# Decode attention over a window of the cache: output copies on the vector engine, one q-projection, another order of the last loads

## The chip, the cores and the metric

The kernel runs on one core of a Trainium2 chip. The metric is the device time of one execution in microseconds; for several executions the median is given. Beside these runs there is one profiled execution, with a trace of every engine and DMA queue.

## The reference

It is one decoding step of grouped-query attention over a window of a key and value cache: 32 sequences (B), one query position, width D = 512, 32 query heads (H) on 8 key/value heads (G), head size 128, cache length 2048. Only the last W = 512 positions are used. All tensors are bf16.

```python
W = min(4096, max(256, Sk // 4))                      # 512
q = (x @ wq).reshape(B, Sq, Hq, Dh)                   # to (B, Hq, 1, Dh)
k = repeat(k_cache[:, :, Sk - W:, :], 4 per head)
v = repeat(v_cache[:, :, Sk - W:, :], 4 per head)
p = softmax((q @ k^T) * Dh ** -0.5)
out = (p @ v).reshape(B, Sq, Hq * Dh) @ wo            # (32, 1, 512)
```

Per sequence 1 MB of K and 1 MB of V are read; wq and wo are 4 MB each. Together it is 75.5 MB.

## The kernel before

The program is written by hand for each engine: each engine runs a fixed list of instructions in order, and semaphores tie the lists together. The sequences are numbered b = 0 to 31 and grouped in 8 blocks kb of four (`NBLK`).

**Loads.** SP issues every load on one queue. K goes into 4 slots (`NK`), V into 10 (`NV`). The order is x, K0, wq, then K(b) and V(b-3) by turns (`VLAG = 3`), wo after V7, and at the end V29, V30, V31. `load_k(b)` waits until the transposes of sequence b-4 are done, and `load_v(b)` until pv of sequence b-10 is done. wo overwrites wq in `wbuf`; `load_wo` waits until the q-projection is over and evacuated.

**Front.** x is transposed on TensorE. `qproj(half)` computes q for 16 heads each, as 64 matmuls into the one PSUM bank `m_ps`; `qt_evac(half)` on ScalarE scales it and copies it into `qT_sb`. The bank holds (head, sequence), `qT_sb` holds (sequence, head), so the copy writes with a step of 32 elements. The second half waits on PE until the first has been evacuated.

**For each sequence s.** TensorE transposes K of sequence s+2 (`transposes`, 32 transposes of 128x128 in four groups). VectorE evacuates three groups into `kT_sb` and ScalarE one (`evac`). `scores(s)` multiplies 8 weight tiles `L` with the transposed K and adds up four sequences in one PSUM half of `sc_ps`, so that 128 partitions hold 4 sequences x 32 heads. `lcopy(blk)` on VectorE puts the q of a block into the places of `L` that aren't zero.

**For each block kb.** VectorE takes the maximum and its negation (`max_block`), ScalarE the exponential with its sum (`exp_block`), VectorE normalises (`norm_block`), TensorE transposes the probabilities (`ptrans`), ScalarE evacuates them (`pt_evac`), and TensorE multiplies with V (`pv`, 128 matmuls of 4 columns). `ot_evac(kb)` copies the result, 128 columns of `m_ps`, into `oT_sb`; this runs on ScalarE and writes with a step of 32 elements, since `oT_sb` holds (head, sequence). At the end `oproj` adds up 32 matmuls of 512 columns, with `oT_sb[:, h * B:(h + 1) * B]` as weights and wo as moving operand, and `out_evac` on ScalarE copies the result out.

**Where the order is set.** TensorE's order is one loop over s = 0 to 39: `transposes(s+2)`, `scores(s)`, then `ptrans(kb)` at s = 4kb+4 and `pv(kb)` at s = 4kb+5. So pv(6) comes at s = 29, between scores(29) and scores(30), and ptrans(7) and pv(7) come at s = 32 and 33. VectorE and ScalarE have loops over b with tasks before and after the evacuations of b: `ot_evac(kb)` before those of b = 4kb+8, `max_block(kb)` and `exp_block(kb)` after those of b = 4kb+5, `norm_block(kb)` before those of b = 4kb+6.

Of the kernel before, what the change touches and what calls it, by code (L numbers as in the profile page):

```python
# [5 lines left out]
B = 32  # L6
D = 512
H = 32
# [25 lines left out]
def bass_standalone__sliding_block_cached__sampling_kernel(  # L34
# [9 lines left out]
    with ExitStack() as ctx:  # L44
# [7 lines left out]
        L = [sb(f"L{i}", [128, 32 * 128], BF16) for i in range(2)]  # L52
        qT_sb = sb("qT_sb", [128, B * H], BF16)
        x_sb = sb("x_sb", [128, D], BF16)
# [4 lines left out]
        pT_sb = [sb(f"pT{i}", [128, W], BF16) for i in range(2)]  # L59
        oT_sb = sb("oT_sb", [128, H * B], BF16)  # L60
        out_sb = sb("out_sb", [128, D], BF16)
# [24 lines left out]
        sem_act_pT = sem("sem_act_pT")  # L86
        sem_act_oT = sem("sem_act_oT")
        sem_act_misc = sem("sem_act_misc")
        sem_dve_kT = sem("sem_dve_kT")
        sem_dve_sm = sem("sem_dve_sm")  # L90
        sem_dve_P = sem("sem_dve_P")
        sem_dve_L = sem("sem_dve_L")
        sem_dve_loc = sem("sem_dve_loc")

# [13 lines left out]
        @block.sync  # L108
        def _(sp):
            def load_k(b):  # L110
                slot = b % NK
                if b >= NK:
                    sp.wait_ge(sem_pe_kT, 4 * (b - NK) + 4)
                src = k_cache[b, :, SK - W:, :].rearrange("g (p r) d -> p g (r d)", p=128)
                dst = kbuf[slot][:, :].rearrange("p (g x) -> p g x", g=G)
                sp.dma_start(dst, src).then_inc(sem_k[slot], 16)  # L116

            def load_v(b):
                slot = b % NV
                if b >= NV:  # L120
                    sp.wait_ge(sem_pe_pv, b - NV + 1)
                src = v_cache[b, :, SK - W:, :].rearrange("g (p r) d -> p g (r d)", p=128)
                dst = vbuf[slot][:, :].rearrange("p (g x) -> p g x", g=G)
                sp.dma_start(dst, src).then_inc(sem_v[slot], 16)  # L124

            def load_wo():
                sp.wait_ge(sem_pe_misc, 3)
                sp.wait_ge(sem_act_misc, 3)
                sp.dma_start(
                    wbuf[:, :].rearrange("p (h n) -> p h n", h=H),  # L130
                    wo.rearrange("(h p) n -> p h n", p=128),
                ).then_inc(sem_wo, 16)

            sp.dma_start(x_sb[0:B, :], x.rearrange("b o d -> (b o) d")).then_inc(sem_x, 16)
            load_k(0)
            sp.dma_start(  # L136
                wbuf[:, :].rearrange("p (t n) -> p t n", t=DT),
                wq.rearrange("(t p) n -> p t n", p=128),
            ).then_inc(sem_wq, 16)
            for b in range(1, B):  # L140
                load_k(b)
                if b >= VLAG:
                    load_v(b - VLAG)
                if b == WO_AFTER:
                    load_wo()
            for b in range(B - VLAG, B):
                load_v(b)
            sp.wait_ge(sem_act_misc, 4)
            sp.dma_start(out.rearrange("b o d -> (b o) d"), out_sb[0:B, :]).then_inc(sem_out, 16)
            sp.wait_ge(sem_out, 16)  # L150
# [13 lines left out]
        def _(pe):  # L164
# [6 lines left out]

            def qproj(half):
                if half == 0:
                    pe.wait_ge(sem_wq, 16)
                    pe.wait_ge(sem_act_misc, 1)
                else:
                    pe.wait_ge(sem_act_misc, 2)
                for hh in range(16):
                    h = 16 * half + hh
                    for t in range(DT):  # L180
                        ins = pe.matmul(  # L181
                            m_ps[:, hh * B:(hh + 1) * B],
                            wbuf[:, t * (H * DH) + h * DH: t * (H * DH) + (h + 1) * DH],
                            xT_sb[:, t * B:(t + 1) * B],
                            start=(t == 0),
                            stop=(t == DT - 1),
                        )
                ins.then_inc(sem_pe_misc, 1)
# [18 lines left out]
            def scores(b):  # L207
                blk, bl = divmod(b, 4)
                half = blk % 2
                if bl == 0:  # L210
                    pe.wait_ge(sem_dve_L, blk + 1)
                    if blk >= 2:
                        pe.wait_ge(sem_act_exp, blk - 1)
                for g in range(G):
                    n = 4 * b + g // 2
                    if g % 2 == 0:
                        pe.wait_ge(evac_sem(n), evac_count(n))
                    ins = pe.matmul(  # L218
                        sc_ps[:, half * 512:(half + 1) * 512],
                        L[blk % 2][:, (bl * 8 + g) * 128:(bl * 8 + g + 1) * 128],  # L220
                        kT_sb[b % NKT][:, g * W:(g + 1) * W],
                        start=(bl == 0 and g == 0),
                        stop=(bl == 3 and g == G - 1),
                    )
                ins.then_inc(sem_pe_scb, 1)
# [9 lines left out]
            def pv(kb):  # L235
                pe.wait_ge(sem_act_pT, kb + 1)
                reg = kb % 4
                if kb == 0:
                    pe.wait_ge(sem_act_misc, 3)
                if kb >= 4:  # L240
                    pe.wait_ge(sem_act_oT, kb - 3)
                for bl in range(4):
# [14 lines left out]
            def oproj():  # L257
                pe.wait_ge(sem_act_oT, NBLK)
                pe.wait_ge(sem_wo, 16)
                pe.wait_ge(sem_act_exp, NBLK - 1)  # L260
                for h in range(H):
                    ins = pe.matmul(  # L262
                        sc_ps[0:B, 0:512],
                        oT_sb[:, h * B:(h + 1) * B],
                        wbuf[:, h * D:(h + 1) * D],
# [7 lines left out]
            transposes(1)  # L273
            qproj(0)
            qproj(1)
            for s in range(0, B + 8):
# [4 lines left out]
                for kb in range(NBLK):  # L281
                    if s == 4 * kb + 3 + LAG1:
                        ptrans(kb)
                    if s == 4 * kb + 3 + LAG2:
                        pv(kb)
# [3 lines left out]
        def _(act):  # L289
# [3 lines left out]

            def qt_evac(half):
                act.wait_ge(sem_pe_misc, 2 + half)
                act.activation(  # L296
                    qT_sb[:, :].rearrange("p (b h) -> p h b", b=B)[:, 16 * half:16 * half + 16, :],
                    m_ps[:, :].rearrange("p (h b) -> p h b", h=16),
                    ACTF.Copy,
                    scale=scale,  # L300
                ).then_inc(sem_act_misc, 1)

# [36 lines left out]

            def ot_evac(kb):  # L340
                act.wait_ge(sem_pe_pv, 4 * kb + 4)
                if kb >= 1:
                    act.wait_ge(sem_act_oT, kb)
                reg = kb % 4
                act.activation(  # L345
                    oT_sb[:, :].rearrange("p (h b) -> p b h", h=H)[:, 4 * kb:4 * kb + 4, :],
                    m_ps[:, reg * 128:(reg + 1) * 128].rearrange("p (b h) -> p b h", b=4),
                    ACTF.Copy,
                ).then_inc(sem_act_oT, 1)

            def out_evac():
                act.wait_ge(sem_pe_misc, 4)
                act.activation(out_sb[0:B, :], sc_ps[0:B, 0:512], ACTF.Copy).then_inc(sem_act_misc, 1)  # L353

            def block_tasks_pre(b):
                for kb in range(NBLK):
                    if b == 4 * kb + 5 + LAG2 + 1:
                        ot_evac(kb)

# [9 lines left out]
            evac(1, 3)  # L369
            qt_evac(0)  # L370
            qt_evac(1)
            for b in range(2, B):
# [3 lines left out]
            for b in range(B, B + 12):  # L376
                block_tasks_pre(b)
                block_tasks_post(b)
            out_evac()

        @block.vector
        def _(dve):
# [16 lines left out]
            def lcopy(blk):  # L399
                if blk == 0:  # L400
                    dve.wait_ge(sem_act_misc, 3)
                    dve.wait_ge(sem_pool, 4)
# [3 lines left out]
                dst = bass.AP(L[blk % 2], 0, [[32 * 128, 128], [1056, 4], [132, 8], [1, 4]])  # L406
                src = bass.AP(qT_sb, blk * 128, [[B * H, 128], [32, 4], [4, 8], [1, 4]])
                dve.tensor_copy(dst, src).then_inc(sem_dve_L, 1)  # L408
# [11 lines left out]
            def norm_block(kb):  # L420
# [6 lines left out]
                dve.tensor_scalar(P_sb[kb % 2][:, :], E_sb[:, :], rs[kb % 2][:, 0:1], None, ALU.mult).then_inc(sem_dve_P, 1)  # L427

            def E(b):
                for c in range(3):  # L430
                    evac(b, c)

            def block_tasks_pre(b):
                for kb in range(NBLK):
                    if b == 4 * kb + 6:
                        norm_block(kb)

            def block_tasks_post(b):
# [10 lines left out]
            for b in range(2, B):  # L449
                block_tasks_pre(b)  # L450
                E(b)
                block_tasks_post(b)
            for b in range(B, B + 8):
                block_tasks_pre(b)
                block_tasks_post(b)


# [26 lines left out]
```

## Time and profile before

| | |
|---|---|
| median of 6 runs | 243.61 us (241.43 to 245.88) |
| profiled execution | 242.48 us |
| its span, from the first to the last instruction | 240.4 us |
| mean granted TensorE clock | 0.844 |
| PE / weight loads busy | 177.6 us / 136.0 us |
| VectorE / ScalarE busy | 74.8 us / 56.5 us |
| HBM read | 75.53 MB, mean 314 GB/s over the span |
| K load, from issue to landing (median) | 12.0 us |
| longest waits | ScalarE for K transposes 104.5 us, VectorE for them 65.2 us, PE for K loads 49.3 us |

The span lies 2.1 us under the time of the same execution. Busy times are sums of instruction durations; matmuls overlap, so a busy PE isn't one at its peak. "PEld" is the weight load of a matmul, which has a row of its own. A wait is the idle time of an engine ahead of an instruction, with what ended it. "The chain that ended last" follows the work back from the last instruction, at each step to what released it.

### The profile page before, as it was taken

How to read it: one execution, taken by the hardware profiler on the slowest of the kernel's cores; microseconds unless marked ns; L12 is line 12 of the kernel's file. 1: busy time of each engine (PE TensorE's matmuls, PEld its weight loads, DVE VectorE, ACT ScalarE, POOL GpSimd, SP SyncE). 2: the span in 40 equal slices, each digit the busy share in tenths (PEclk: the TensorE clock that was granted, in tenths of full speed). 3: DMA queues.
4: the chain of work that ended last, by engine and by line, in shares of the span. 5: the costliest groups of instructions: out<-in, count | busy, mean ns of one | idle time of the engine just before them, and what ended most of it. 6: DMA issues, size and time to landing. Idle time of an engine off the chain costs nothing.

```text
span 240.4 us, 5498 instructions
## 1 busy us (share of the span) xinstructions
PE 177.6 (74%) x2477; PEld 136.0 (57%) x2500; DVE 74.8 (31%) x136; ACT 56.5 (24%) x69; POOL 7.6 (3%) x8
## 2 busy tenths in 40 slices
PE   0506599969981059996958699869986998497695
PEld 0506577657750056874946478647854785284632
DVE  0303054640460030365315413641364136131100
ACT  2100543412240001242203212221232123211200
POOL 8300000000000000000000000000000000000000
PEclk9965789987897557799979977987798779889769
DMA  6999999999999999999999999999999999993000
GB/s 202 423 386 348 350 348 350 349 348 348 350 350 348 349 348 350 350 348 350 350 348 348 349 348 350 348 348 349 348 348 350 348 348 348 345 341 110 3 3 5
DMA packets 71320, 75.92 MB, mean 316 GB/s; under 512 B 1089, under 2 KB 70785, under 8 KB 70785
## 3 DMA queue, kind: packets, MB, share of 16 engines
q1 hardware_dynamic: 71296, 75.57, 97.8%
q8 instruction: 20, 0.33, 0.6%
q14 instruction: 4, 0.02, 0.0%
HBM read 75.53 MB, written 0.03 MB: 314 GB/s over the span
## 4 chain that ended last, share of the span: by engine, by line
DMA 56%; PE 37%; ACT 2%; SPq 2%; issue 1%; DVE 1%; DVEq 0%
DMA kbuf<-in_k_cache_dram 56%; PE kT_ps L204 16%; PE m_ps L248 8%; PE sc_ps L218 8%; PE sc_ps L262 4%; PE m_ps L181 1%; SPq L124 1%; ACT qT_sb L296 1%; ACT oT_sb L345 0%; DVE mx L416 0%; SPq L116 0%; ACT pT L338 0%; ACT out_sb L353 0%; SPq L136 0%; DVE P L427 0%
## 5 line engine op out<-in xcount | busy, mean ns | idle before, releaser
L204 PE MATMUL kT_ps<-ident,kbuf 128*128 128x128 bf16 x1024 | 81.2, 253 | 49.3 <-DMA kbuf<-in_k_cache_dram 49.3
L204 PEld LDWEIGHTS kT_ps<-ident,kbuf 128*128 128x128 bf16 x1024 | 76.1, 116 | 56.4 <-DMA kbuf<-in_k_cache_dram 54.5
L394 DVE COPY kT<-kT_ps 128x1024 bf16<-128x1024 bf16 x96 | 62.6, 686 | 116.1 <-PE kT_ps L204 65.2
L218 PE MATMUL sc_ps<-kT,L 128*128 128x512 bf16 x233 | 60.8, 401 | 1.8 <-DVE kT L394 0.4
L312 ACT ACTIVATE kT<-kT_ps 128x1024 bf16<-128x1024 bf16 x32 | 32.7, 1023 | 111.9 <-PE kT_ps L204 104.5
L218 PEld LDWEIGHTS sc_ps<-kT,L 128*128 128x128 bf16 x256 | 25.0, 103 | 26.6 <-issue 5.6
L248 PEld LDWEIGHTS m_ps<-pT,vbuf 128*128 128x128 bf16 x1024 | 27.1, 97 | 2.5 <-ACT pT L338 0.9
L248 PE MATMUL m_ps<-pT,vbuf 128*128 128x4 bf16 x1024 | 27.2, 165 | 0.7 <-ACT pT L338 0.7
L345 ACT ACTIVATE oT_sb<-m_ps 128x128 bf16<-128x128 f32 x8 | 5.8, 730 | 34.7 <-PE m_ps L248 34.7
L416 DVE TENSOR_REDUCE mx<-sc_ps 128x1 f32<-128x512 f32 x8 | 5.5, 691 | 16.6 <-PE sc_ps L218 16.6
L262 PE MATMUL sc_ps<-wbuf,oT_sb 128*32 128x512 bf16 x32 | 8.9, 448 | 0.8 <-ACT oT_sb L345 0.8
L324 ACT ACTIVATE E_sb<-sc_ps,nmx 128x512 f32<-128x512 f32 x8 | 5.5, 687 | 14.6 <-DVE nmx L418 14.6
L262 PEld LDWEIGHTS sc_ps<-wbuf,oT_sb 128*32 128x32 bf16 x32 | 3.5, 111 | 5.9 <-issue 2.5
L338 ACT ACTIVATE pT<-pT_ps 128x512 bf16<-128x512 bf16 x8 | 4.8, 597 | 7.4 <-PE pT_ps L232 7.4
L181 PE MATMUL m_ps<-xT_sb,wbuf 128*128 128x32 bf16 x128 | 3.7, 185 | 2.5 <-ACT qT_sb L296 2.5
L296 ACT ACTIVATE qT_sb<-m_ps 128x512 bf16<-128x512 f32 x2 | 4.8, 2406 | 2.6 <-PE m_ps L181 2.6
L181 PEld LDWEIGHTS m_ps<-xT_sb,wbuf 128*128 128x128 bf16 x128 | 3.6, 102 | 2.6 <-ACT qT_sb L296 2.6
L232 PEld LDWEIGHTS pT_ps<-ident,P 128*128 128x128 bf16 x32 | 2.4, 98 | 4.6 <-DVE P L427 3.0
L232 PE MATMUL pT_ps<-ident,P 128*128 128x128 bf16 x32 | 3.1, 219 | 2.5 <-DVE P L427 2.5
L408 DVE COPY L<-qT_sb 128x128 bf16<-128x128 bf16 x8 | 1.5, 188 | 8.6 <-ACT qT_sb L296 8.6
L427 DVE TENSOR_SCALAR P<-E_sb,rs 128x512 bf16<-128x512 f32 x8 | 3.9, 487 | 0.3
L160 POOL MEMSET L<- 128x4096 bf16 x1 | 3.5, 3511 | 0.0
(15 smaller groups left out, 11.1 us busy)
## 6 DMA issues: line engine op xcount, KB each, us to landing
kbuf<-in_k_cache_dram SPq DMA_DIRECT2D x32, 1024.0 KB, 12.0
vbuf<-in_v_cache_dram SPq DMA_DIRECT2D x32, 1024.0 KB, 12.0
wbuf<-in_wq_dram SPq DMA_DIRECT2D x1, 4096.0 KB, 15.2
wbuf<-in_wo_dram SPq DMA_DIRECT2D x1, 4096.0 KB, 20.9
x_sb<-in_x_dram SPq DMA_DIRECT2D x1, 32.0 KB, 1.8
out_dram<-out_sb SPq DMA_DIRECT2D x1, 32.0 KB, 1.5
```

Source lines behind the costliest of these rows:

```text
L181: ins = pe.matmul(m_ps[:, hh * B:(hh + 1) * B], wbuf[:, t * (H * DH) + h * DH: t * (H * DH) + (h + 1) * DH], xT_sb[:, t * B:(t + 1) * B], ...
L204: ins = pe.transpose(dst, src, ident[:, :])
L218: ins = pe.matmul(sc_ps[:, half * 512:(half + 1) * 512], L[blk % 2][:, (bl * 8 + g) * 128:(bl * 8 + g + 1) * 128], kT_sb[b % NKT][:, g * W ...
L232: ins = pe.transpose(pT_ps[:, j * 128:(j + 1) * 128], P_sb[kb % 2][:, j * 128:(j + 1) * 128], ident[:, :])
L248: ins = pe.matmul(m_ps[:, reg * 128 + bl * 32 + 4 * g: reg * 128 + bl * 32 + 4 * g + 4], vbuf[vslot][:, g * W + j * 128: g * W + (j + 1) * ...
L262: ins = pe.matmul(sc_ps[0:B, 0:512], oT_sb[:, h * B:(h + 1) * B], wbuf[:, h * D:(h + 1) * D], start=(h == 0), stop=(h == H - 1),)
L296: act.activation(qT_sb[:, :].rearrange("p (b h) -> p h b", b=B)[:, 16 * half:16 * half + 16, :], m_ps[:, :].rearrange("p (h b) -> p h b", ...
L312: act.activation(kT_sb[b % NKT][:, c * 1024:(c + 1) * 1024], kT_ps[:, bank * 1024:(bank + 1) * 1024], ACTF.Copy,).then_inc(sem_act_kT, 1)
L324: act.activation(E_sb[:, :], sc_ps[:, half * 512:(half + 1) * 512], ACTF.Exp, bias=nmx[kb % 2][:, 0:1], scale=1.0, accum_out=ssum[kb % 2][ ...
L345: act.activation(oT_sb[:, :].rearrange("p (h b) -> p b h", h=H)[:, 4 * kb:4 * kb + 4, :], m_ps[:, reg * 128:(reg + 1) * 128].rearrange("p ...
L394: dve.tensor_copy(kT_sb[b % NKT][:, c * 1024:(c + 1) * 1024], kT_ps[:, bank * 1024:(bank + 1) * 1024],).then_inc(sem_dve_kT, 1)
L416: dve.tensor_reduce(mx[kb % 2][:, 0:1], sc_ps[:, half * 512:(half + 1) * 512], AXX, ALU.max).then_inc(sem_dve_loc, 1)
```

## The change

It has these parts:

- The q-projection is done in one go: 128 matmuls into both banks of `sc_ps` (1024 f32 columns), and one `qt_evac` on ScalarE. `qT_sb` now holds (head, sequence), so the copy is plain. `lcopy` reads `qT_sb` with a step of 32 elements instead.
- `ot_evac` and `out_evac` move from ScalarE to VectorE. `oT_sb` now holds (sequence, head), so that copy is plain too; `oproj` reads its weights from `oT_sb` with a step of 32 elements instead.
- SP's order is built as a list, and K31 is put directly behind K30, ahead of V27.
- On TensorE pv(6) moves from s = 29 to s = 31, behind scores(31). Its `ot_evac(6)` on VectorE comes at b = 33, ahead of the tasks after b = 33, among which is `max_block(7)`.

```diff
 # SP
-            for b in range(1, B):
-                load_k(b)
-                if b >= VLAG:
-                    load_v(b - VLAG)
-                if b == WO_AFTER:
-                    load_wo()
-            for b in range(B - VLAG, B):
-                load_v(b)
+            for b in range(1, B):
+                order.append(("k", b))
...
+            order.remove(("k", B - 1))
+            order.insert(order.index(("k", B - 2)) + 1, ("k", B - 1))
...
 # TensorE
-            def qproj(half):
+            def qproj():
...
-                            m_ps[:, hh * B:(hh + 1) * B],
+                            sc_ps[:, h * B:(h + 1) * B],
...
             def pv(kb):
-                    pe.wait_ge(sem_act_oT, kb - 3)
+                    pe.wait_ge(sem_dve_oT, kb - 3)
...
             def oproj():
-                        oT_sb[:, h * B:(h + 1) * B],
+                        bass.AP(oT_sb, h, [[B * H, 128], [H, B]]),
...
-                    if s == 4 * kb + 3 + LAG2:
+                    pv_at = 4 * kb + 3 + LAG2
+                    if kb == NBLK - 2:
+                        pv_at = B - 1
+                    if s == pv_at:
                         pv(kb)
 # ScalarE
-            def qt_evac(half):
-                act.wait_ge(sem_pe_misc, 2 + half)
-                act.activation(
-                    qT_sb[:, :].rearrange("p (b h) -> p h b", b=B)[:, 16 * half:16 * half + 16, :],
-                    m_ps[:, :].rearrange("p (h b) -> p h b", h=16),
-                    ACTF.Copy,
-                    scale=scale,
-                ).then_inc(sem_act_misc, 1)
+            def qt_evac():
+                act.wait_ge(sem_pe_misc, 2)
+                act.activation(qT_sb[:, :], sc_ps[:, :], ACTF.Copy, scale=scale).then_inc(sem_act_misc, 1)
...
-            def ot_evac(kb):
...
-            def out_evac():
...
 # VectorE
             def lcopy(blk):
-                src = bass.AP(qT_sb, blk * 128, [[B * H, 128], [32, 4], [4, 8], [1, 4]])
+                src = bass.AP(qT_sb, blk * 4, [[H * B, 128], [1, 4], [4 * B, 8], [B, 4]])
...
+            def ot_evac(kb):
+                dve.wait_ge(sem_pe_pv, 4 * kb + 4)
+                if kb >= 1:
+                    dve.wait_ge(sem_dve_oT, kb)
+                reg = kb % 4
+                dve.tensor_copy(oT_sb[:, kb * 128:(kb + 1) * 128], m_ps[:, reg * 128:(reg + 1) * 128]).then_inc(sem_dve_oT, 1)
+
+            def out_evac():
+                dve.wait_ge(sem_pe_misc, 3)
+                dve.tensor_copy(out_sb[0:B, :], sc_ps[0:B, 0:512]).then_inc(sem_dve_out, 1)
...
             def block_tasks_pre(b):
                 for kb in range(NBLK):
                     if b == 4 * kb + 6:
                         norm_block(kb)
+                    ot_at = 4 * kb + 5 + LAG2 + 1
+                    if kb == NBLK - 2:
+                        ot_at = B + 1
+                    if b == ot_at:
+                        ot_evac(kb)
```

More of the change, by code (lines that the diff above doesn't have):

```diff
@@ L52, in bass_standalone__sliding_block_cached__sampling_kernel @@
         L = [sb(f"L{i}", [128, 32 * 128], BF16) for i in range(2)]
-        qT_sb = sb("qT_sb", [128, B * H], BF16)
+        qT_sb = sb("qT_sb", [128, H * B], BF16)
         x_sb = sb("x_sb", [128, D], BF16)
@@ L59, in bass_standalone__sliding_block_cached__sampling_kernel @@
         pT_sb = [sb(f"pT{i}", [128, W], BF16) for i in range(2)]
-        oT_sb = sb("oT_sb", [128, H * B], BF16)
+        oT_sb = sb("oT_sb", [128, B * H], BF16)
         out_sb = sb("out_sb", [128, D], BF16)
@@ L86, in bass_standalone__sliding_block_cached__sampling_kernel @@
         sem_act_pT = sem("sem_act_pT")
-        sem_act_oT = sem("sem_act_oT")
         sem_act_misc = sem("sem_act_misc")
@@ L92, in bass_standalone__sliding_block_cached__sampling_kernel @@
         sem_dve_L = sem("sem_dve_L")
+        sem_dve_oT = sem("sem_dve_oT")
+        sem_dve_out = sem("sem_dve_out")
         sem_dve_loc = sem("sem_dve_loc")
@@ L126, in load_wo @@
             def load_wo():
-                sp.wait_ge(sem_pe_misc, 3)
-                sp.wait_ge(sem_act_misc, 3)
+                sp.wait_ge(sem_pe_misc, 2)
+                sp.wait_ge(sem_act_misc, 2)
                 sp.dma_start(
@@ L139, in _ @@
             ).then_inc(sem_wq, 16)
+            order = []
             for b in range(1, B):
-                load_k(b)
+                order.append(("k", b))
                 if b >= VLAG:
-                    load_v(b - VLAG)
+                    order.append(("v", b - VLAG))
                 if b == WO_AFTER:
+                    order.append(("wo", 0))
+            for b in range(B - VLAG, B):
+                order.append(("v", b))
+            order.remove(("k", B - 1))
+            order.insert(order.index(("k", B - 2)) + 1, ("k", B - 1))
+            assert len(order) == len(set(order)) == 2 * B
+            for kind, b in order:
+                if kind == "k":
+                    load_k(b)
+                elif kind == "v":
+                    load_v(b)
+                else:
                     load_wo()
-            for b in range(B - VLAG, B):
-                load_v(b)
-            sp.wait_ge(sem_act_misc, 4)
+            sp.wait_ge(sem_dve_out, 1)
             sp.dma_start(out.rearrange("b o d -> (b o) d"), out_sb[0:B, :]).then_inc(sem_out, 16)
@@ L170, in xT @@
                 ins.then_inc(sem_pe_misc, 1)
-            def qproj(half):
[L173 to L179, printed above, removed]
+            def qproj():
+                pe.wait_ge(sem_wq, 16)
+                pe.wait_ge(sem_act_misc, 1)
+                for h in range(H):
                     for t in range(DT):
                         ins = pe.matmul(
-                            m_ps[:, hh * B:(hh + 1) * B],
+                            sc_ps[:, h * B:(h + 1) * B],
                             wbuf[:, t * (H * DH) + h * DH: t * (H * DH) + (h + 1) * DH],
@@ L211, in scores @@
                     pe.wait_ge(sem_dve_L, blk + 1)
+                    if blk == 0:
+                        pe.wait_ge(sem_act_misc, 2)
                     if blk >= 2:
@@ L237, in pv @@
                 reg = kb % 4
-                if kb == 0:
-                    pe.wait_ge(sem_act_misc, 3)
                 if kb >= 4:
-                    pe.wait_ge(sem_act_oT, kb - 3)
+                    pe.wait_ge(sem_dve_oT, kb - 3)
                 for bl in range(4):
@@ L257, in oproj @@
             def oproj():
-                pe.wait_ge(sem_act_oT, NBLK)
+                pe.wait_ge(sem_dve_oT, NBLK)
                 pe.wait_ge(sem_wo, 16)
@@ L273, in _ @@
             transposes(1)
-            qproj(0)
-            qproj(1)
+            qproj()
             for s in range(0, B + 8):
@@ L338, in pt_evac @@
                 act.activation(pT_sb[kb % 2][:, :], pT_ps[:, 0:W], ACTF.Copy).then_inc(sem_act_pT, 1)
-            def ot_evac(kb):
[L341 to L349, printed above, removed]
-            def out_evac():
-                act.wait_ge(sem_pe_misc, 4)
-                act.activation(out_sb[0:B, :], sc_ps[0:B, 0:512], ACTF.Copy).then_inc(sem_act_misc, 1)
             def block_tasks_pre(b):
-                for kb in range(NBLK):
-                    if b == 4 * kb + 5 + LAG2 + 1:
-                        ot_evac(kb)
+                pass
             def block_tasks_post(b):
@@ L369, in _ @@
             evac(1, 3)
-            qt_evac(0)
-            qt_evac(1)
+            qt_evac()
             for b in range(2, B):
@@ L378, in _ @@
                 block_tasks_post(b)
-            out_evac()
         @block.vector
@@ L400, in lcopy @@
                 if blk == 0:
-                    dve.wait_ge(sem_act_misc, 3)
+                    dve.wait_ge(sem_act_misc, 2)
                     dve.wait_ge(sem_pool, 4)
@@ L452, in _ @@
                 block_tasks_post(b)
-            for b in range(B, B + 8):
+            for b in range(B, B + 12):
                 block_tasks_pre(b)
                 block_tasks_post(b)
+            out_evac()
 _INS = ['x', 'k_cache', 'v_cache', 'wq', 'wo']
```

## The prediction, made before the changed kernel was run

> **What bounds the kernel now.** I read three views in this order: the slices of the page, the chain of work that ended last, and the timeline of the last 50 us. First the slices (40 of them, 6 us each):
>
> ```profile
> PEclk9965789987897557799979977987798779889769
> DMA  6999999999999999999999999999999999993000
> GB/s 202 423 386 348 350 348 350 349 348 348 350 350 348 349 348 350 350 348 350 350 348 348 349 348 350 348 348 349 348 348 350 348 348 348 345 341 110 3 3 5
> ```
>
> From the fourth slice to slice 36 the loads run at about 349 GB/s without a hole. The TensorE rows of the waits view say the same from the other side: PE waits 49.3 us in all for kbuf. So until about 220 us the kernel is a copy from HBM, and work saved there only makes PE wait longer. After the last load there is a tail with no traffic. It is read from the end of the chain (start us, us, what):
>
> ```profile
> 196.03 13.25 DMA kbuf<-in_k_cache_dram
> ...
> 209.32 3.32 PE kT_ps L204 x32
> ...
> 212.65 1.29 PE sc_ps L218 x6
> ...
> 214.37 3.19 PE m_ps L248 x128
> ...
> 217.63 3.41 PE sc_ps L218 x15
> ...
> 221.07 0.70 DVE mx L416
> ...
> 224.62 3.50 PE m_ps L248 x128
> ...
> 228.15 0.73 ACT oT_sb L345
> ...
> 228.93 8.94 PE sc_ps L262 x32
> ...
> 237.89 0.59 ACT out_sb L353
> ```
>
> K of sequence 31 lands at 209.28. Behind it stand its transposes, scores(29), all of pv(6), scores(30) and (31), the softmax of block 7, pv(7), the output projection and the copy out. The last V is not in this chain: its issue began at 209.5 and landed 11.6 us later, at 221.1, before pv(7) starts. **The tail hangs on when K31 lands, not on when the loads end.** The timeline shows what fills the queue and PE before that:
>
> ```profile
> 193.08 2.90 SPq L124 DMA_DIRECT2D vbuf<-in_v_cache_dram  x1
> 196.03 2.79 SPq L116 DMA_DIRECT2D kbuf<-in_k_cache_dram  x1
> 202.10 1.96 PE L204 MATMUL kT_ps<-ident,kbuf 128*128 128x128 bf16 x32 [1.10 <-DMA kbuf<-in_k_cache_dram]
> 205.62 0.39 PE L232 MATMUL pT_ps<-ident,P 128*128 128x128 bf16 x4
> 209.32 3.32 PE L204 MATMUL kT_ps<-ident,kbuf 128*128 128x128 bf16 x32 [3.31 <-DMA kbuf<-in_k_cache_dram]
> ```
>
> V27 is issued at 193.08 and lands 12.0 us later, at 205.1; K31 is next. PE idles 3.31 us for it.
>
> **Part 1, the front: merged q-projection, plain qT copy, lcopy.** Two strided ScalarE copies of 2.41 us, with PE idle 2.5 us between the halves, become one plain copy of 1024 columns, 1.02 us by the row of the 1024-column kT evacuation. Scores(0) start some 3.5 us earlier than 32.44. I cost this at nothing: wq, K1, K2 and K3 have long been issued then, and the later issues stand back to back (K6 at 32.82 follows V2's, which began at 29.86 and took 2.92), so no load starts sooner. PE then waits longer for K4, K5 and on. If loads were not the bound, the 3.5 us would be a gain. `lcopy` now reads qT with a step of 32 elements: between today's 0.19 us and 0.73 us (the strided ScalarE row below), eight times, in idle VectorE time (busy 31%); uncovered it could cost 8 x 0.54 = 4.3 us, but each runs many microseconds ahead of its block's scores. load_wo's two waits end earlier and it stands behind ten loads: nothing.
>
> **Part 2, oT and out copies from ScalarE to VectorE.** The row of L345 is 730 ns. VectorE has no such copy in the trace. Its rows are 691 ns for reducing 512 f32 from PSUM and 686 ns for copying 1024 bf16; one f32 column per 1.04 ns and a fixed 0.155 us fit the first, so 128 columns are 0.29 us. Bounds: 0.22 (twice that rate) and 0.73 (no better than ScalarE). For blocks 0 to 5 the copy stands ahead of E(4kb+8) on VectorE and waits for pv(kb), but on PE pv(kb) is issued before the transposes that E needs, so the evacuations behind it lose no time: after the pv that ended at 192.75 the next one started at 193.72. The last one is on the path: 0.73 becomes 0.29, **-0.44**. The copy to out_sb, 512 f32 columns, takes 0.69 by the reduction's row against 0.59 on ScalarE: **+0.10** (0.42 to 0.73 as bounds).
>
> **Part 3, the output projection reads oT with a step.** Its weights, [128 x 32], now step 32 elements (64 bytes) from column to column. No strided weight load is in the trace. The nearest row is ScalarE's strided writes with that step: 2406 ns for 512 and 730 ns for 128 columns, 4.36 ns a column; plain ScalarE copies (597 for 512, 1023 for 1024) make 0.83. [...] By the row a load would be 32 x (4.36 - 0.83) = 0.11 us longer than its 97 ns, 0.21 us. Laid open it costs 32 x 0.11 = 3.6 us. But in the last 5 us of the projection one matmul ends every 0.216 us (22 loads over 4.63 us in the timeline) and the loads already run beside the previous matmul, so 0.21 us just fits. I take 0 (bounds 0 and +3.6; a gain is excluded, since the loads are hidden already).
>
> **Part 4, K31 before V27.** The order by index is now K30, K31, V27 to V31. SP issues K31 at 193.08 instead of 196.03. Its wait is for the transposes of sequence 27, which ended at 187.1, so nothing behind it on SP is held. It lands where V27 did, at 205.1; V27 where K31 did, at 209.28; V28 to V31 as before (212.2, 215.0, 218.0, 221.1).
>
> **Part 5, pv(6) behind scores(31), and its copy ahead of max_block(7).** PE now goes: ptrans(6) ends 206.01. Transposes(31) start at 206.05, since K31 is there. They take 1.96, not 3.32: the slow ones ran at a granted clock of 0.5 after the idle 3.3 us, and now there is no idle. Scores(29) 1.89, to 209.9; scores(30) and (31) 3.41, to 213.3. V27 is there, so pv(6) runs 3.19, to 216.5. On VectorE the new copy of pv(6) is *in front of* max_block(7). So the max, its negation, the exponential, the normalisation, ptrans(7) and pv(7) all queue behind it although the scores were ready at 213.3: moving pv(6) off PE's path puts it back through VectorE. Copy 0.29, to 216.85. From the start of the max to the start of pv(7) the chain took 3.55 (221.07 to 224.62): pv(7) starts at 220.4. All but V31 have landed, and its quarter comes at 223.0: no wait. pv(7) 3.50, to 223.9; copy 0.29; projection from 224.3 instead of 228.93.
>
> **Sum.** K31 earlier, 209.32 - 206.05 = 3.27; transposes(31) at full clock, 1.36; the copy in front of the max, -0.33; last copy, +0.44; out copy, -0.10: **4.6 us**. The span goes from 240.4 to 235.8. The profiled execution took 242.48, 2.1 more than its span, so it would take 237.9. It lies 1.1 below the median of the six runs, 243.61; taken from that median, 4.6 us leave **239.0**.
>
> [...] The granted clock, microsecond by microsecond, is 0.5 from 225.9 to 232.7 and 1.0 after, so the projection spent its first 3.8 us at half rate and took 8.94, where 32 x 0.216 is 6.9. All changes near the end sit on one grid of 3.41 us (191.7, 195.1, 208.8, 212.2, 225.9, 232.7). [...] By the row I keep 8.94. [...]
>
> **Rivals.**
> (a) *K31 doesn't land earlier*, because the queue holds it back. Then the chain is today's plus 0.33 minus 0.44 plus 0.10: 243.6. The back-to-back issues speak against it.
> (b) *Weight loads laid open*: +3.6, so 242.6. For: the cover fits by a hair. Against: loads stand beside matmuls in this trace.
> (c) *Slower: strided loads neither overlap nor stay short.* Each matmul of the projection then takes 0.216 + 0.097 + 32 x 4.36 ns = 0.45 us, 14.5 for 32, with 2.0 for the cold start 16.5: 7.5 more than today, net +2.9, 246.5. It decides once a matmul with its load takes over (8.94 + 4.6 - 2.0) / 32 = 0.36 us.
> (d) *The softmax is not held by the new copy.* Then V31 sets the end: 221.1 + 0.9 for its quarter is 222.0 instead of 223.9: 237.1. The order on VectorE speaks against it.
>
> **How the numbers follow.** Forecast 0.73, rival (a) 0.07, (b) 0.09, (c) 0.07, (d) 0.04. A measurement of this kernel can tell about 1%, 2.4 us, from no change. Faster by more than that: forecast, (d), and the cheaper half of (b), 0.80; within 1%: 0.13; slower: 0.07. The forecast's own range, with the clock's -1.2 to +0.5, copies up to 0.4 dearer and a median that wanders by some 0.7, is 237.0 to 240.4; to leave out no more than 2 in 10 it goes up to 241.5.
>
> **What would show it.** Right: the waits for kbuf end near 206; no PE idle ahead of transposes(31); pv(6) between scores(31) and ptrans(7); the max of block 7 right after the oT copy at about 216.8; projection from 224.3; loads ending near 220 as now. Wrong: a spacing of over 0.25 us between projection matmuls at full clock, K31 landing after 207, the max starting near 213, or holes in the load rate before slice 34.

## The result and the profile after

The changed kernel takes 238.87 us (median of 10 runs, 237.58 to 240.32); the kernel before takes 243.74 us in the same series. The ratio is 0.982, with a 95% interval of 0.979 to 0.985: about 4.4 us of 243.7 are gone. The medians are over all runs, while the ratio leaves out runs more than 1.5% above the fastest of their kernel, which here only the kernel before has. The forecast was 239.0.

The slices of the page show that the stream of loads is as before, and only the tail behind it is shorter:

```profile
DMA  6999999999999999999999999999999999996000
GB/s 199 425 389 348 349 349 349 349 348 349 348 350 349 347 349 349 350 348 350 348 350 349 349 348 348 349 348 349 350 346 350 347 349 348 349 334 225 4 3 6
```

The rate stays at 349 GB/s from the fourth slice on. A slice is now 5.96 us, so the traffic ends at the same time, near 220 us.

The profiled execution took 240.12 us (span 238.3). That is only 2.4 us below the profiled execution of before, while the medians lie 4.9 apart. A profile is one execution: the one of before was 1.3 us under its median, this one 1.3 us over. I therefore read the changed kernel from two profiles, this one and the one of the repeat (e1). First the end of the chain in this one (start us, us, what):

```profile
202.49 2.44 PE kT_ps L212 x32
204.94 0.22 issue
205.16 2.69 PE sc_ps L228 x7
207.85 0.22 PE pT_ps L242 x4
208.07 1.79 PE kT_ps L212 x32
...
215.04 3.25 PE m_ps L256 x128
...
218.52 0.69 DVE mx L402
...
222.27 3.59 PE m_ps L256 x128
...
226.23 9.50 PE sc_ps L270 x32
```

K31 is no longer in it: its issue began at 193.5 and it landed 12.0 us later, at 205.5, before PE asked for it at 208.07. V27 was issued at 196.4 and landed at 209.4. But transposes(31) still start 2 us later than the 206.05 of the forecast. The lines above them say why: scores(28), L228 at 205.16, take 2.69 us, where they took 1.73 in other profiles, and transposes(30) 2.44 instead of 1.96. The granted clock is 0.5 from 203.8 to 207.2. Ahead of transposes(30), at 202.49, PE had waited 2.34 us for K30.

The groups show the moved copies (busy us, mean ns):

```profile
L420 DVE CAST oT_sb<-m_ps 128x128 bf16<-128x128 f32 x8 | 2.3, 292 | 40.8 <-PE m_ps L256 40.8
...
L270 PEld LDWEIGHTS sc_ps<-wbuf,oT_sb 128*32 128x32 bf16 x32 | 4.4, 141 | 5.1 <-issue 2.9
...
L424 DVE CAST out_sb<-sc_ps 32x512 bf16<-32x512 f32 x1 | 0.7, 678 | 9.6 <-PE sc_ps L270 9.6
...
L394 DVE COPY L<-qT_sb 128x128 bf16<-128x128 bf16 x8 | 2.1, 259 | 4.2 <-ACT qT_sb L306 4.2
```

The oT copy costs 292 ns for the 730 on ScalarE, the out copy 678 for 586, lcopy 259 for 188; a weight load of the projection took 111 on the mean before and takes 141.

### The profile page after: what moved, and what is told of

The parts are those of the page before. It is cut to its first block, busy times and chain, and to the rows that moved or that the text cites. A ratio compares the mean times of both kernels' runs of the same rounds, so it can differ in the third digit from the quotient of the medians.

```text
span 238.3 us, 5498 instructions
## 1 busy us (share of the span) xinstructions
PE 165.7 (70%) x2478; PEld 124.5 (52%) x2500; DVE 77.3 (32%) x145; ACT 46.4 (19%) x59; POOL 7.6 (3%) x8
## 5 line engine op out<-in xcount | busy, mean ns | idle before, releaser
L212 PE MATMUL kT_ps<-ident,kbuf 128*128 128x128 bf16 x1024 | 69.8, 231 | 60.4 <-DMA kbuf<-in_k_cache_dram 57.7
L212 PEld LDWEIGHTS kT_ps<-ident,kbuf 128*128 128x128 bf16 x1024 | 64.1, 104 | 68.8 <-DMA kbuf<-in_k_cache_dram 65.1
L380 DVE COPY kT<-kT_ps 128x1024 bf16<-128x1024 bf16 x96 | 61.1, 684 | 89.4 <-issue 47.8
L228 PE MATMUL sc_ps<-kT,L 128*128 128x512 bf16 x234 | 59.3, 393 | 3.2 <-issue 2.0
L317 ACT ACTIVATE kT<-kT_ps 128x1024 bf16<-128x1024 bf16 x32 | 32.8, 1024 | 143.8 <-PE kT_ps L212 126.2
L228 PEld LDWEIGHTS sc_ps<-kT,L 128*128 128x128 bf16 x256 | 24.8, 102 | 27.2 <-issue 4.8
L420 DVE CAST oT_sb<-m_ps 128x128 bf16<-128x128 f32 x8 | 2.3, 292 | 40.8 <-PE m_ps L256 40.8
L270 PEld LDWEIGHTS sc_ps<-wbuf,oT_sb 128*32 128x32 bf16 x32 | 4.4, 141 | 5.1 <-issue 2.9
L424 DVE CAST out_sb<-sc_ps 32x512 bf16<-32x512 f32 x1 | 0.7, 678 | 9.6 <-PE sc_ps L270 9.6
L172 POOL MEMSET L<- 128x4096 bf16 x1 | 3.5, 3512 | 0.0
L173 POOL MEMSET L<- 128x4096 bf16 x1 | 3.5, 3512 | 0.0
L409 DVE RECIPROCAL rs<-ssum 128x1 f32<-128x1 f32 x8 | 1.3, 164 | 6.8 <-ACT E_sb L329 6.8
L394 DVE COPY L<-qT_sb 128x128 bf16<-128x128 bf16 x8 | 2.1, 259 | 4.2 <-ACT qT_sb L306 4.2
```

The costliest lines, as they stand in the source:

```text
L172: pool.memset(L[0][:, :], 0.0).then_inc(sem_pool, 1)
L212: ins = pe.transpose(dst, src, ident[:, :])
L228: ins = pe.matmul(sc_ps[:, half * 512:(half + 1) * 512], L[blk % 2][:, (bl * 8 + g) * 128:(bl * 8 + g + 1) * 128], kT_sb[b % NKT][:, g * W ...
L270: ins = pe.matmul(sc_ps[0:B, 0:512], bass.AP(oT_sb, h, [[B * H, 128], [H, B]]), wbuf[:, h * D:(h + 1) * D], start=(h == 0), stop=(h == H - 1),
L317: act.activation(kT_sb[b % NKT][:, c * 1024:(c + 1) * 1024], kT_ps[:, bank * 1024:(bank + 1) * 1024], ACTF.Copy,).then_inc(sem_act_kT, 1)
L380: dve.tensor_copy(kT_sb[b % NKT][:, c * 1024:(c + 1) * 1024], kT_ps[:, bank * 1024:(bank + 1) * 1024],).then_inc(sem_dve_kT, 1)
```

## The experiments

Theory: the gain is the earlier landing of K31, and the rest of the change moves the end by less than half a microsecond. Rivals: the copies, the merged q-projection or the later pv(6) bring it. The first four kernels ran on one chip, with a median of 243.1 us for the kernel before.

### e1: the changed kernel again

> The changed kernel once more, for a second profile and a shared baseline. Time: 4.4 to 4.9 us below the kernel before. If the profiled execution's smaller gain (2.4 us) came from where the half-clock windows happened to fall (scores(28) and the whole projection start), this profile has the same landings of K30, K31 and V27 (relative to each other) but other half-clock windows, and its tail differs by 1 to 2 us. If instead the change itself costs something that the prediction left out, scores(28) and transposes(31) are again late, starting near 207.9.

Measured 238.66 us, ratio 0.985 (0.981 to 0.988). The chain of its profile:

```profile
202.34 1.96 PE kT_ps L212 x32
204.30 1.73 PE sc_ps L228 x8
206.03 0.22 PE pT_ps L242 x4
206.25 1.79 PE kT_ps L212 x32
208.04 5.18 PE sc_ps L228 x24
213.22 3.20 PE m_ps L256 x128
...
216.65 0.69 DVE mx L402
...
220.41 3.59 PE m_ps L256 x128
...
224.37 9.38 PE sc_ps L270 x32
```

Here the clock is 1.0 at scores(28), and the tail is the one of the forecast: transposes(31) at 206.1, scores(31) done at 213.2, projection from 224.37 (forecast 224.3). Two further profiles of the same kernel, e8 and e11, show both cases. In e11 the clock is 1.0 there, and the projection starts at 224.27. In e8 it starts at 226.29: the clock is 0.5 from 202.9 to 206.3, which this time falls on transposes(30) and not on scores(28):

```profile
202.63 3.38 PE kT_ps L212 x32
206.01 0.22 issue
206.23 1.73 PE sc_ps L228 x7
```

So the late start in the first profile isn't a cost of the change but 1.9 us that come and go between executions, with a half-clock stretch of 3.4 us just ahead of transposes(31).

### e2: the kernel before, with K31 ahead of V27

```diff
-                load_k(b)
+                if b < B - 1:
+                    load_k(b)
+                if b == B - 2:
+                    load_k(B - 1)
```

> The kernel before with one edit: K31 is loaded ahead of V27. Theory (the tail hangs on when K31 lands): transposes(31) start near 206, scores(29) end near 210, V27 has landed by then (209.3), so pv(6) in its old place does not wait, scores(31) end near 216.5, the softmax of block 7 starts at once because the copy of pv(6) is on ScalarE: 239 us, all of the gain. Rival (the later pv(6) is what makes the earlier K31 worth anything, or the copies bring the gain): at most 1.5 us faster than before.

Measured 239.43 us, ratio 0.986 (0.982 to 0.990). Within what these runs can tell, this one edit brings what the whole change brings (e1 0.985, 238.66 us; a rest of up to about 1 us isn't excluded). Its chain, also with half clock, from 203.1 to 206.5, on transposes(30) and scores(28):

```profile
207.88 1.79 PE kT_ps L207 x32
209.66 1.73 PE sc_ps L221 x8
211.39 3.19 PE m_ps L251 x128
214.58 3.49 PE sc_ps L221 x16
218.07 0.02 issue
218.09 0.70 DVE mx L419
```

pv(6) stands at its old place, between scores(29) and scores(30), and doesn't wait for V27. The max starts at 218.09, against 218.52 and 218.57 in the two profiles of the changed kernel with a half-clock stretch at that place. Moving pv(6) behind scores(31) gained nothing, since the copy in front of the max put its length back. The pair e3 and e4 below, which differ in this alone, says the same: 243.05 and 243.08 us.

### e3: the changed kernel, K31 again behind V27

```diff
-            order.remove(("k", B - 1))
-            order.insert(order.index(("k", B - 2)) + 1, ("k", B - 1))
```

> The changed kernel with K31 put back behind V27. Theory: PE idles until K31 lands near 209.3 again, and the rest of the chain is as long as before (+0.33 copy in front of the max, -0.44 last copy, +0.10 out copy): 243.5 to 244 us, no gain. Rival (the copies, the merged q-projection or the later pv(6) bring the gain): 239 to 241.

Measured 243.05 us, ratio 1.001 (0.997 to 1.004): the gain is gone. In its chain a K load ends at 209.75, just ahead of transposes(31) at 209.79, and the projection starts at 228.07. One thing is not as the forecast has it. PE idles as long for K31 as before, and yet these transposes run at full clock; in e4, after nearly the same idle time, they run at half clock as in the kernel before. First e3, then e4:

```profile
209.79 1.96 PE L210 MATMUL kT_ps<-ident,kbuf 128*128 128x128 bf16 x32 [3.45 <-DMA kbuf<-in_k_cache_dram]
```

```profile
209.90 3.25 PE L210 MATMUL kT_ps<-ident,kbuf 128*128 128x128 bf16 x32 [3.54 <-DMA kbuf<-in_k_cache_dram]
```

So the slow transposes(31) are not a fixed price of the late K31 but one that some executions pay. From transposes(31) to the projection e3 and e1 both take 18.3 us; they differ in when K31 lets transposes(31) start, by 3.7 us.

### e4: only the merged q-projection and the copies on VectorE

The changed kernel without the two lines of e3 and without `pv_at` and `ot_at` for block 6.

> The changed kernel without its tail edits: K31 behind V27, pv(6) and its copy where they were; left are the merged q-projection and the copies on VectorE with strided weight loads. Theory: only the last copy (-0.44) and the out copy (+0.10) are on the path: 243.4 us, the same as before within 0.5. Rival (the 3.5 us saved at the front count): 240. Rival (strided weight loads cost): up to 247.

Measured 243.08 us, ratio 1.001 (0.997 to 1.004). Front, copies and strided weight loads together cost and gain nothing that shows.

### e5 and e10: the max ahead of the copy

```diff
-                    pe.wait_ge(sem_dve_oT, kb - 3)
+                    pe.wait_ge(sem_dve_oT, kb if kb == NBLK - 1 else kb - 3)
...
-                        ot_at = B + 1
+                        ot_at = B + 3
```

The copy of pv(6) comes behind the normalisation of block 7 on VectorE. In the changed kernel pv(7) came after this copy because the max was queued behind it; here a wait of its own on PE keeps pv(7) behind the copy.

> The changed kernel with the copy of pv(6) behind the normalisation of block 7 on VectorE, and pv(7) waiting for that copy on PE. Theory (the copy in front of the max holds the softmax for the length of pv(6)): the max starts when scores(31) end, near 213.3 instead of 216.7; the softmax runs beside pv(6); then the landing of V31 (221.1 to 221.5) is what is late, its quarter of pv(7) ends near 222.3 instead of 224.0: 1.7 us faster than the changed kernel, about 237. Rival (the softmax is hidden anyway or something else holds pv(7)): as the changed kernel, 238.8.

> The kernel with the max first once more, beside the changed kernel. If its lead of 3.4 us over the changed kernel is the softmax set free (1.7 us) and luck with the half-clock windows around scores(28) for the rest, the lead is now 1 to 2.5 us, its time 236.5 to 238. If the whole 3.4 us belong to the edit, 236.6 again with the changed kernel at 239 to 240.

Measured 236.63 us, ratio 0.976 (0.971 to 0.980), and 236.92 us, ratio 0.974 (0.969 to 0.978). The changed kernel beside them on the same chips took 240.0 (e8) and 238.8 (e11), so the lead is 3.4 and 1.9 us. e8 ran with half clock at transposes(30) in its profile, so part of the 3.4 is probably that (five of its six runs took about 240, one 238.1; only one was profiled); the 1.9 agrees with the 1.7 of the theory. **This version beats both kernels.** The timeline of e5 shows the softmax beside pv(6) (start us, us, engine, line):

```profile
212.78 3.36 PE L256 MATMUL m_ps<-pT,vbuf 128*128 128x4 bf16 x128
...
212.98 0.69 DVE L402 TENSOR_REDUCE mx<-sc_ps 128x1 f32<-128x512 f32 x1 [4.58 <-PE sc_ps L228]
...
219.47 2.73 PE L256 MATMUL m_ps<-pT,vbuf 128*128 128x4 bf16 x97 [1.21 <-issue]
...
222.58 8.83 PE L270 MATMUL sc_ps<-wbuf,oT_sb 128*32 128x512 bf16 x32 [0.38 <-DVE oT_sb L420]
```

The max starts at 212.98 instead of 216.65 in e1: 3.7 us earlier. The projection starts at 222.58 instead of 224.37: only 1.8 us earlier. V31 landed at about 221.0 (issued at 209.4, 11.6 us), so its quarter of pv(7), 0.9 us, could not end much before 221.9. It ended at 222.2. The remaining 0.3 us go to a stop of 1.21 us between the first and the second quarter of pv(7) that the profile puts down to nothing (see e9).

### e6: the same, with matmuls to keep the clock up

```diff
+                    if b >= B - 2:
+                        for _ in range(5 if b == B - 2 else 6):
+                            pe.matmul(sc_ps[:, 0:512], ident[:, :], kT_sb[0][:, 0:512], start=True, stop=True)
```

> The same with 11 additional matmuls of 512 columns whose result nobody reads, 5 ahead of the third and 6 ahead of the last quarter of pv(7), where PE would wait for V30 and V31. Theory (the projection runs 2 to 2.5 us over its 6.9 us because the granted clock is 0.5 at its start): the clock stays at 1.0, the projection takes 6.9 to 7.3, 2 us faster than without: about 235. Rival (the projection is slow for another reason, its strided weights for instance): same as without, or later by what the 2.4 us of matmuls don't find as idle time.

Measured 239.55 us, ratio 0.989 (0.984 to 0.993): 2.9 us *slower* than e5. The expected gain failed; that the half clock makes the projection long held. Its timeline:

```profile
221.29 1.91 PE L255 MATMUL sc_ps<-kT,ident 128*128 128x512 bf16 x4 [0.24 <-issue]
...
223.89 2.67 PE L255 MATMUL sc_ps<-kT,ident 128*128 128x512 bf16 x6
...
227.73 7.12 PE L273 MATMUL sc_ps<-wbuf,oT_sb 128*32 128x512 bf16 x32 [0.38 <-DVE oT_sb L423]
```

The projection takes 7.12 us instead of 8.83, since the clock is 1.0 from 226.4 on. So the half clock is what makes the projection long, and its strided weights are not. But the clock had dropped at 216.1, before the first added matmul: pv(6), with 128 matmuls of 4 columns, did not keep it up. Nor did the added matmuls shorten the stretch of half clock: it lasted 10.2 us in e5 (215.9 to 226.1) and 10.2 us here (216.1 to 226.4), and the projection merely started after it. The added matmuls ran at about 0.45 us each, not 0.216, stood in front of a V that had long landed, and held pv(7) up by more than they won.

### e7: the projection's weights without a step

```diff
-                        bass.AP(oT_sb, h, [[B * H, 128], [H, B]]),
+                        oT_sb[:, h * B:(h + 1) * B],
...
-                dve.tensor_copy(oT_sb[:, kb * 128:(kb + 1) * 128], m_ps[:, reg * 128:(reg + 1) * 128])
+                dve.tensor_copy(
+                    oT_sb[:, :].rearrange("p (h b) -> p b h", h=H)[:, 4 * kb:4 * kb + 4, :],
+                    m_ps[:, reg * 128:(reg + 1) * 128].rearrange("p (b h) -> p b h", b=4),
+                )
```

> The changed kernel with oT in its old layout: the projection's weights have no step again, and the VectorE copies write with a step of 32 elements. If strided weight loads are hidden (a load of 133 ns beside a matmul of 216), the projection takes as long as now, and the two copies on the path cost 0 to 0.44 us more each: 238.8 to 239.7. If they are laid open, up to 1.2 us faster (32 x 36 ns).

> The changed kernel beside the three on the same chip: 4.4 us below the kernel before, its profile's projection between 7.7 and 9.5 us depending on where the half-clock windows fall.

Measured 239.53 us, ratio 0.988 (0.983 to 0.993), beside 240.0 us, 0.989 (0.983 to 0.994), for the changed kernel (e8). No difference shows. What the two do in the trace, first the loads of the changed kernel in its first profile, then those and the copy of e7 (ns min/median/max):

```profile
L270 PEld LDWEIGHTS sc_ps<-wbuf,oT_sb x32: 131/133/158, 226.2 to 235.1; 128*32 128x32 bf16 x32
```

```profile
L270 PEld LDWEIGHTS sc_ps<-wbuf,oT_sb x32: 97/97/152, 226.8 to 235.3; 128*32 128x32 bf16 x32
...
L420 DVE CAST oT_sb<-m_ps x8: 712/720/727, 57.8 to 226.0; 128x128 bf16<-128x128 f32 x8
```

A step of 64 bytes makes a weight load 36 ns longer, which the matmul beside it hides: at full clock one matmul of the projection ends every 216 ns in both, and the projection takes 9.11 us in e7 and 9.03 in e8. On a *write* the step is dear on VectorE too, 720 ns for 292. Of the oT copy's gain of 0.44 us, then, nearly all comes from the plain layout and not from the other engine.

### e9: where does PE stop for no shown reason?

```diff
-                for h in range(H):
+                for h in [0, 0, 0, 0, 0] + list(range(H)):
```

> As the kernel with the max first, with the first four matmuls of the q-projection issued five more times (20 matmuls with their loads, in time that is hidden by loads). It is about two stops of PE that the profile puts down to nothing (issue): in that kernel one of 1.7 us after 25 or 26 transposes of sequence 2, one of 1.2 us after 32 matmuls of pv(7). If PE stops because its own instructions are late (a place in the instruction stream), both stops move some 20 matmuls forward: after about 6 transposes of sequence 2, after about 12 matmuls of pv(7). If a semaphore is late (V29 for the second), the second stop stays at 32. Time as the kernel with the max first, 236.6.

It is e5 with 20 more matmuls ahead in PE's list. Measured 238.55 us, ratio 0.980 (0.971 to 0.990), not the 236.6 expected; all four runs (237.8 to 239.1) lie above the median of e5. In its profile K30 landed 1.2 us later than in e5 and transposes(30) and scores(28) fell into half clock, so transposes(31) start at 209.83. The front of e5 and then of e9:

```profile
26.27 1.56 PE L212 MATMUL kT_ps<-ident,kbuf 128*128 128x128 bf16 x25
...
29.51 0.55 PE L212 MATMUL kT_ps<-ident,kbuf 128*128 128x128 bf16 x7 [1.69 <-issue]
```

```profile
26.92 0.44 PE L212 MATMUL kT_ps<-ident,kbuf 128*128 128x128 bf16 x5
...
29.82 1.67 PE L212 MATMUL kT_ps<-ident,kbuf 128*128 128x128 bf16 x27 [2.46 <-issue]
```

The stop came after 25 transposes and now comes after 5: 20 further forward, as many as were added. It belongs to a place in PE's instruction list and not to a tile or a semaphore; waits of the program stand only at every eighth transpose. Half of the expectation failed: the second stop, in pv(7), did not move forward but was gone. In e6 and e10 it stood after the first 31 matmuls, 1.28 and 1.59 us long. The program has a wait for V29 at that place, but in e5 V29 had landed at 215.0.

The traces say more on both stops. They have a queue of instruction loads beside the data, 20 packets of 16 KB in an execution, each taking about 1 us. In e5 one packet runs from 26.9 to 28.1 and one from 217.1 to 218.2. The second is the only one that the DMA view shows between 216 and 219 (packets, MB, share of 16 engines):

```profile
q8 instruction: 1, 0.02, 2.3%
```

PE goes on at 29.5 and 219.5, 1.4 and 1.3 us after these packets. In every profile of the changed kernel and of e5, e6, e9 and e10 the stop in the front ends 1.4 to 1.6 us after the end of such a packet, and the stop in pv(7) 1.3 to 1.4. Where pv(7) started 1.8 us or more after its packet (the changed kernel, e9), it didn't stop. So late instructions are by far the likeliest cause of both: with the softmax freed, pv(7) starts so early that PE's idle time no longer covers the instruction load. No run moved a packet alone, so this is not shown to the end.

The same queue may bear on K31. Near the end one load lands every 3.0 us, but in the kernel before K31 lands 4.2 us after V27, and an instruction packet (206.1 to 207.2) falls into that gap. In the first profile of the changed kernel the long gap, 3.9 us, stands behind K31, where V27 lands and nothing waits; so some 1.2 us of what the earlier K31 brings is this gap. In e9 the packet comes at 200.6 and the long gap, 4.0 us, comes with it, now ahead of K30. That fits e9's late K30 and a good part of its lost 1.9 us. From 85 us on the thirteen traces have 26 gaps of over 3.6 us, and a packet begins in 25 of them; but most packets fall into ordinary gaps, so what makes these few long stays open.

### e11: the changed kernel beside e10

> The changed kernel beside it: 238.7 to 240.0. Transposes(31) start near 206.1 where scores(28) run at full clock, near 207.9 where they run at half clock.

Measured 238.8 us, ratio 0.982 (0.978 to 0.986). In its profile scores(28) ran at full clock, and transposes(31) start at 206.0.

## Why the prediction was right

- **What bounds the kernel.** Right. K31's landing decides: e2 alone gains what the change gains, e3 loses it.
- **Part 1, front.** Right that it is worth nothing (e4). The 3.5 us at scores(0) were 2.2, since PE now stops on its way, 1.85 us among the transposes of sequence 2 (see e9). Hidden all the same.
- **Part 2, copies.** 0.29 and 0.69 forecast, 0.292 and 0.678 measured. The fit through the reduction's row held.
- **Part 3, strided weights.** Right to take 0: a load of 133 ns stands beside a matmul of 216. The estimate from ScalarE's strided writes, 0.21 us for a load, was too high; the step adds 36 ns and not 0.11 us. Rivals (b) and (c) fall with that. By the column this read by TensorE pays 1.1 ns (36 ns for 32), a third of what a write by ScalarE (3.5 ns) or VectorE (3.3 ns) pays.
- **Part 4.** K31 at 205.5 (forecast 205.1), V27 at 209.4 (209.28), V31 at 221.5 (221.1). Right; rival (a) falls.
- **Part 5.** Right in e1 and e11 to 0.1 us. The step that was incomplete is "now there is no idle": there is none ahead of transposes(31), but PE still waits for K30, 2.3 us in three of the four profiles of the changed kernel. In two of these half clock follows on transposes(30) or scores(28) and makes most of the 1.9 us. The forecast put the clock's chance into the projection and not there. And the 1.36 us for transposes(31) at full clock was counted as sure: e3 has them at full clock without the gain. What is sure is the earlier start, 3.3 us in the forecast and 3.7 between e3 and e1.
- **The queue behind the copy.** Right, and the point of e5: free the max, and V31 is next, as rival (d) had it. It was forecast at 237.1 and measured at 236.6 and 236.9, by an edit.
- **The projection.** I kept 8.94; the four profiles have 9.50, 9.38, 9.03 and 9.91. The cold start, a clock of 0.5 as it begins, is the reason, as e6 shows (7.12 at a clock of 1.0). The term was 0.1 to 1.0 us too small. No run shows the -1.2 to +0.5 us that the range takes for the clock, nor the 7.7 us at the low end of e8's expectation; the four profiles showed +0.1 to +1.0 against 8.94. The edges of the 3.41 us grid lie elsewhere in each execution: the half rate ended at 232.7 before and at 231.1 in the first profile of the changed kernel. In all twelve profiles other than e6 it lasted from the projection's start to the next edge and one whole stretch of 3.41 us more: 0.5 + 3.4 in e8 (9.03), 2.3 + 3.4 in e11 (9.91). Full rate from the next edge on never came.
- **The number.** That 239.0 and 238.87 agree so closely is luck. Executions of the changed kernel spread from 237.6 to 240.3, the 1.36 us are not sure, and the projection was longer than put down. The gain of 4.4 to 4.9 us is more than the 3.7 of the earlier start; the rest is probably the clock on the average of many executions, but the few profiles don't show how often it falls where.

## What to carry to other kernels

In a kernel that loads without a hole, look at what each of the last transfers still has to go through, and load those with the longest way first: here one swapped pair of 1 MB loads is the whole gain that shows. A wait taken off one engine's list may come back through another's, as here with the max of block 7 behind the copy of pv(6) (216.65 in e1, 212.98 in e5): see what is queued behind each instruction that now waits later. And take more than one profile of a kernel whose tail depends on a clock that comes and goes: here two profiles of one program differ by 2 us at the start of the last stage.

## What the runs showed of the hardware

- A step of 64 bytes costs 36 ns on a TensorE weight load of 32 columns (97 to 133 ns), but on a copy's write 3.3 ns a column on VectorE (292 to 720 ns for 128), about as much as the 3.5 ns of ScalarE's rows before.
- In two profiles matmuls of 4 columns did not hold the clock: it fell to 0.5 at 215.9 in e5 and at 216.1 in e6, near the end of a pv that had kept PE busy since 212.8 and 213.3.
- The projection began at a clock of 0.5 and kept it for the rest of the running stretch of the 3.41 us grid and one whole stretch more, in all twelve profiles other than e6: 3.9 us in e8, 5.7 us in e11.
- PE can stop for 1.2 to 2.5 us with no wait in the program that would explain it. In the front the place moves with the count of the instructions ahead of it, and PE goes on 1.3 to 1.6 us after a 16 KB packet of the instruction queue has ended.
- Near the end of the loads one landing follows the last after 3.0 us, but after 4.2 (before) and 4.0 us (e9) where an instruction packet at 206.1 and at 200.6 falls between. Most packets show no such gap, and the cause is open.
